# Block 0's attention scores as 18 full bursts instead of 24 bursts of three, two and four chunks

## Chip, cores, metric

One core of a Trainium2 chip runs the whole program. The metric is device time in microseconds (us), the median of several executions. Besides whole-run times I use lengths between two marks in one trace; the text says which.

## The reference, cut to what matters

```python
h   = x + attention(layernorm(x), wqkv, wo)   # S=2048, D=1024, 32 heads of 32, causal window 256
out = h + silu(layernorm(h) @ w1) @ w2        # F=3584
# mask: 0 <= q - k < 256; softmax over k
```

The kernel works on four blocks of 512 queries. A head's scores are computed in chunks of 128 keys by 128 queries. A query tile of a later block sees three key tiles, which makes 12 chunks for four query tiles. Block 0 has nothing before it and only nine: (k,q) = (0,0) (0,1) (0,2) (1,1) (1,2) (1,3) (2,2) (2,3) (3,3).

## The kernel before

TensorE alternates between two kinds of work: the dense projections (Q, K and V) of block b, and the attention of block b-1. Four heads make a group; each head has 32 rows, so a score burst uses TensorE as four row tiles of 32 rows side by side (`tile_position`). It writes two tiles of two banks each (`sc`, one for each pair of heads) in PSUM, the memory that takes the results of matmuls. ScalarE takes exponentials of them into one of 12 buffers, GpSimd zeroes the masked triangles, and a later attention output multiplies by V.

```python
PIECES = {"A": [(0, 0, 3, 0), (-2, 0, 1, 3)],     # (key tile, first query tile, how many, chunk place)
          "B": [(-1, 0, 2, 0), (2, 2, 2, 2)],
          "C": [(3, 3, 1, 0), (1, 1, 3, 1)]}      # block 0 skips key tiles below 0: 3, 2 and 4 chunks

def scores(b, g, kind):
    for kt, q0, nq, ch in PIECES[kind]:
        ...
        for hh in range(4):                       # four heads, four row tiles
            nc.tensor.matmul(sc[hh // 2][:, hh % 2, ch*P:(ch+nq)*P], lhsT=kT..., rhs=qT...,
                             start=True, stop=True, tile_position=(hh * 32, 0))
    for pair in range(2):
        nc.scalar.activation(out=e[:, :, lo:hi], in_=sc[pair][:, :, lo:hi], func=ACT.Exp, scale=scale)
        mask(...)                                 # GpSimd

for g in range(8):                                # 24 places for each block
    for kind in "ABC":
        run_late()
        scores(b - 1, g, kind)
        dense[n]()                                # eight matmuls of 512 columns
        if pending: pending.pop(0)()              # a third of the last group's attention output
        ...
    pending = tail_of(b - 1, g)                   # 5, 6 and 5 of 16 products
```

The softmax here doesn't subtract the row's maximum and nothing guards it: scores larger than these inputs give would overflow.

Of the kernel before, what the change touches and what calls it, by code (L numbers as in the profile page):

```python
# [11 lines left out]
ACT = mybir.ActivationFunctionType  # L12
ALU = mybir.AluOpType

P = 128
# [11 lines left out]
CHUNKS = [  # L27
    [(-2, "A", 3), (-1, "B", 0), (0, "A", 0)],
    [(-1, "B", 1), (0, "A", 1), (1, "C", 1)],
    [(0, "A", 2), (1, "C", 2), (2, "B", 2)],  # L30
    [(1, "C", 3), (2, "B", 3), (3, "C", 0)],
]
KINDS = "ABC"


@with_exitstack
def kernel(
# [10 lines left out]
    nc = tc.nc  # L48
# [6 lines left out]
    DH = D // H  # L55
# [3 lines left out]
    NB = S // 512  # L59
    G = H // 4  # L60
    VW = DH + 1
    scale = float(DH) ** -0.5
# [20 lines left out]
    sc = [sc_pool.tile([P, 2, 512], F32, name=f"sc{i}") for i in range(2)]  # L83
    o_ps = [ps.tile([P, 8, 64], F32, name=f"o_ps{i}") for i in range(2)]
# [23 lines left out]
    qT = [view(r_a, (4096, 8192, 12288, 0)[b], G, 512) for b in range(NB)]  # L108
    kT = [view(r_a, 16384 + 4096 * b, G, 512) for b in range(NB)]
    v = view(r_a, 32768, S // P, H, VW)  # L110
# [4 lines left out]
    ebuf = [view(r_e, 1024 * i, 2, 512) for i in range(12)]  # L115
# [10 lines left out]
    def load_x(b, j):  # L126
        nc.sync.dma_start(out=x_ring[(b % 2) * 4 + j], in_=x2d[(b * 4 + j) * P:(b * 4 + j + 1) * P, :])
# [72 lines left out]
    def ln_tiles(tag):  # L200
        st = small.tile([P, 4, 2], F32, name=f"st_{tag}", tag=f"st_{tag}")
        rs = small.tile([P, 4], F32, name=f"rs_{tag}", tag=f"rs_{tag}")
        return st, rs
# [5 lines left out]
    def next_acc():  # L209
        acc_n[0] += 1  # L210
        return acc_banks[acc_n[0] % len(acc_banks)]

    def v_group(b, j, c, copy):
        acc = next_acc()
        for kt in range(KT):
            nc.tensor.matmul(acc, lhsT=lnT_b[b % 2][:, kt, j * P:(j + 1) * P], rhs=wv[:, kt, c * 512:(c + 1) * 512],  # L216
                             start=(kt == 0), stop=(kt == KT - 1))
        copy(out=v[:, b * 4 + j, c * 16:(c + 1) * 16, 0:DH], in_=acc.rearrange("p (h d) -> p h d", d=DH))

    def qk_group(b, which, g, copy):  # L220
        acc = next_acc()
        col0 = which * D + g * P
        for kt in range(KT):
            nc.tensor.matmul(acc, lhsT=wqk[:, kt, col0:col0 + P], rhs=lnT_b[b % 2][:, kt, :],  # L224
                             start=(kt == 0), stop=(kt == KT - 1))
        copy(out=(qT, kT)[which][b][:, g, :], in_=acc)  # L226
# [7 lines left out]
    late = []  # L234

    def run_late():
        while late:
            late.pop(0)()
# [12 lines left out]
    def e_of(i, kind, pair):  # L251
        return ebuf[(i * 6 + KINDS.index(kind) * 2 + pair) % 12]

    def scores(b, g, kind):
        for kt, q0, nq, ch in PIECES[kind]:
            t = b * 4 + kt
            if t < 0:
                continue
            for hh in range(4):
                r0 = hh * DH  # L260
                nc.tensor.matmul(  # L261
                    sc[hh // 2][:, hh % 2, ch * P:(ch + nq) * P],
                    lhsT=kT[t // 4][r0:r0 + DH, g, (t % 4) * P:(t % 4 + 1) * P],
                    rhs=qT[b][r0:r0 + DH, g, q0 * P:(q0 + nq) * P],
                    start=True, stop=True, tile_position=(r0, 0),
                )
        lo, hi = 0, 512
        if b == 0:
            lo, hi = {"A": (0, 384), "B": (256, 512), "C": (0, 512)}[kind]
        for pair in range(2):  # L270
            e = e_of(b * G + g, kind, pair)
            nc.scalar.activation(out=e[:, :, lo:hi], in_=sc[pair][:, :, lo:hi], func=ACT.Exp, scale=scale)  # L272
            if kind == "A":
                mask(e, 0, 1, True)
                mask(e, 2, 1 if b == 0 else 2, False)
            elif kind == "B":
                if b > 0:
                    mask(e, 1, 1, False)
                mask(e, 2, 1, True)
            else:  # L280
                mask(e, 0, 2, True)
                mask(e, 3, 1, False)

    def mask(e, c0, n, upper):
        ap = e[:, :, c0 * P:(c0 + n) * P].rearrange("p h (c q) -> p h c q", q=P)
        sgn = 1 if upper else -1
        nc.gpsimd.affine_select(out=ap, in_=ap, pattern=[[0, 2], [0, n], [sgn, P]],  # L287
                                compare_op=ALU.is_ge if upper else ALU.is_gt,
                                fill=0.0, base=0, channel_multiplier=-sgn)

    def attn_out(b, g, first, last):
        i = b * G + g
        for n in range(first, last):
            pair, qt, hh = n // 8, n // 2 % 4, n % 2
            chunks = [x for x in CHUNKS[qt] if b * 4 + x[0] >= 0]
            for m, (kt, kind, ch) in enumerate(chunks):
                nc.tensor.matmul(  # L297
                    o_ps[pair][:, qt * 2 + hh, 0:VW],
                    lhsT=e_of(i, kind, pair)[:, hh, ch * P:(ch + 1) * P],
                    rhs=v[:, b * 4 + kt, g * 4 + pair * 2 + hh, :],  # L300
                    start=(m == 0), stop=(m == len(chunks) - 1),
                )
            if n % 8 == 7:
                attn_norm(i, pair)

    def attn_norm(i, pair):
        recip = small.tile([P, 8, 1], F32, name="recip", tag="recip")
        nc.vector.reciprocal(out=recip[:], in_=o_ps[pair][:, :, DH:VW])
        nc.vector.tensor_tensor(
            out=obuf[i % 3][:, :, pair * 64:(pair + 1) * 64].rearrange("p t (h d) -> p t h d", d=DH),  # L310
            in0=o_ps[pair][:, :, 0:DH].rearrange("p (t h) d -> p t h d", h=2),
            in1=recip[:].rearrange("p (t h) o -> p t h o", h=2).to_broadcast([P, 4, 2, DH]), op=ALU.mult,
        )

    def attn_transpose(b, g):
        i = b * G + g
        nc.sync.dma_start_transpose(out=qT[b][:, g, :].rearrange("p (t q) -> p t q", q=P),
                                    in_=obuf[i % 3].rearrange("p t d -> p (t d)"))
# [7 lines left out]
    dve, act = nc.vector.tensor_copy, nc.scalar.copy  # L326
# [24 lines left out]
    def ln1_steps(b):  # L351
        st, rs = ln_tiles("a")
        xs = [x_ring[(b % 2) * 4 + j] for j in range(4)]
        steps = [lambda j=j: ln_stats(xs[j], st, j) for j in range(4)]
        steps += rstd_steps(st, rs)
        for j in range(4):
            steps.append(lambda j=j: ln_norm(xs[j], st, rs, j))
        return steps, [lambda j=j: ln_transpose(xs[j], lnT_b[b % 2], j) for j in range(4)]
# [13 lines left out]
    steps = sum(ln1_steps(1), [])  # L372
# [8 lines left out]
        nc.sync.dma_start(out=w1[:, kt, :], in_=w1_v[:, kt, :])  # L381


    pending = []
    for b in range(1, NB):
        dense = [lambda j=j, c=c: v_group(b, j, c, dve) for j in range(4) for c in range(2)]
        dense += [lambda w=w, g=g: qk_group(b, w, g, dve) for g in range(G) for w in range(2)]
        if b + 1 < NB:
            for j in range(4):
                load_x(b + 1, j)  # L390
            steps, turns = ln1_steps(b + 1)
        else:
            steps, turns = [], []
            nc.sync.dma_start(out=wo[:, 0:4, :], in_=wo_v[:, 0:4, :])
            nc.sync.dma_start(out=wo[:, 4:8, :], in_=wo_v[:, 4:8, :])
            load_res(0)
            load_res(1)
        n = 0
        for g in range(G):
            for kind in KINDS:  # L400
                run_late()
                if b == NB - 1 and n in (4, 10, 14):
                    load_w1({4: 7, 10: 6, 14: 5}[n])
                scores(b - 1, g, kind)
                dense[n]()
                if pending:
                    pending.pop(0)()
                if steps and n >= 1 and n != 3:
                    steps.pop(0)()
                elif turns and n % 3 == 2:  # L410
                    turns.pop(0)()
                n += 1
            pending = tail_of(b - 1, g)
        assert not steps and not turns


    dense = []
# [6 lines left out]
    steps = []  # L424
    n = 0
    for g in range(G):
        for kind in KINDS:
            run_late()
# [8 lines left out]
            if n == 9:  # L437
                steps = ln2_steps(0)
# [7 lines left out]
        pending = tail_of(NB - 1, g)  # L446
# [28 lines left out]
    for b in range(NB):  # L475
        extra = []
        if b == 0:
            extra = [(f, 1) for f in pending]
            pending = []
        for ft in range(FT):  # L480
# [8 lines left out]
            if b == 0 and 6 <= ft < 14:  # L489
                j, c = divmod(ft - 6, 2)  # L490
# [4 lines left out]
        steps = ln2_steps(b + 1) if b + 1 < NB else []  # L495
# [55 lines left out]
```

## Time and profile before

| | before |
|---|---|
| median of 3 executions | 699.61 us (699.46 to 699.77) |
| TensorE busy in the profiled execution | 98% of 697.4 us |
| ScalarE, GpSimd busy | 37%, 25% |
| block 0's scores beside block 1's projections | 51.65 to 108.66 us, 57.01 us |
| first score burst to first MLP matmul | 51.65 to 292.51 us, 240.86 us |

Read the busy shares with care: TensorE's 98% includes the time in which the array changes its mode. Differences of starts in the timeline tell more than lengths, for matmul ends are modelled. The lines are in the prediction.

### The profile page before, as it was taken

Reading aid. Unit: us, or ns where it says so; the run is one execution under the profiler, and the core shown is the slowest. Engines: PE = TensorE matmul, PEld = TensorE weight load, DVE = VectorE, ACT = ScalarE, POOL = GpSimd, SP = SyncE. Lnnn points to the kernel's source line nnn. Section 1 sums busy time; section 2 is a strip of 40 time slices with the busy share of each in tenths; the row PEclk is TensorE's granted clock in tenths of the full one; section 3 lists DMA queues with packets and bytes.
Section 4 is the critical chain, followed back from the end, with each engine's and each line's share of the span. In section 5 each row is a group of like instructions: output and inputs, shape, how many; then the busy total and the mean of one; then the engine's idle time right before and its main releaser. Section 6 shows DMA issues by size and latency. Waiting matters only on the chain.

```text
span 697.4 us, 12171 instructions
## 1 busy us (share of the span) xinstructions
PE 686.6 (98%) x4970; PEld 334.9 (48%) x5059; DVE 286.5 (41%) x608; ACT 259.9 (37%) x335; POOL 172.3 (25%) x375
## 2 busy tenths in 40 slices
PE   8999999999999999999999999999999999999998
PEld 3444555555555555544444444444444444444445
DVE  5446645753444348544425233334144251233111
ACT  4316667777777777621310023300033200233000
POOL 1006566777777777600000000000000000000000
PEclk9999999999999999999999999999999999999999
DMA  9541123025431578881023410023300024100110
GB/s 311 171 73 57 32 55 91 17 49 157 116 122 25 180 228 293 211 296 58 32 75 99 105 39 1 0 77 83 83 1 0 10 92 96 46 1 0 31 39 23
DMA packets 75399, 60.55 MB, mean 87 GB/s; under 512 B 49232, under 2 KB 59472, under 8 KB 75344
## 3 DMA queue, kind: packets, MB, share of 16 engines
q1 hardware_dynamic: 75344, 59.78, 29.7%
q8 instruction: 39, 0.64, 0.4%
q14 instruction: 16, 0.13, 0.1%
HBM read 39.85 MB, written 8.39 MB: 69 GB/s over the span
## 4 chain that ended last, share of the span: by engine, by line
PE 97%; DMA 1%; issue 1%; DVE 0%; ACT 0%; SPq 0%
PE hacc L461 18%; PE hacc L498 17%; PE acc L224 16%; PE acc L498 10%; PE acc L461 9%; PE acc L216 8%; PE acc L243 7%; PE o_ps L297 5%; PE sc L261 4%; PE hacc L243 2%; DMA r_o<-in_A_x_dram 1%; PE o_ps L196 0%; DVE ln_st L158 0%; ACT r_w L197 0%; DVE r_o L179 0%
## 5 line engine op out<-in xcount | busy, mean ns | idle before, releaser
L272 ACT ACTIVATE r_e<-sc 128x1024 bf16<-128x1024 f32 (+2 forms) x192 | 175.8, 967 | 66.1 <-PE sc L261 52.5
L287 POOL TENSOR_SCALAR_AFFINE_SELECT r_e<-r_e 128x256 bf16<-128x256 bf16 (+1 forms) x368 | 169.3, 489 | 120.7 <-ACT r_e L272 117.7
L498 PEld LDWEIGHTS <-r_a 128*128 128x128 bf16 x952 | 90.9, 98 | 103.0
L461 PEld LDWEIGHTS <-r_w 128*128 128x128 bf16 x896 | 87.4, 98 | 104.8
L498 PE MATMUL hacc<-r_a 128*128 128x512 bf16 (+2 forms) x605 | 121.9, 359 | 0.6
L461 PE MATMUL hacc<-r_e,r_w 128*128 128x512 bf16 x444 | 100.2, 379 | 0.6
L470 ACT ACTIVATE r_n<-hacc 128x512 f32<-128x512 f32 x30 | 17.9, 597 | 178.9 <-PE hacc L461 178.9
L224 PEld LDWEIGHTS <-r_w 128*128 128x128 bf16 x512 | 46.1, 98 | 58.6 <-issue 8.9
L498 PE MATMUL acc<-r_a 128*128 128x512 bf16 x328 | 73.6, 379 | 0.4
L226 DVE CAST r_a<-acc 128x512 bf16<-128x512 f32 x56 | 38.7, 691 | 81.3 <-PE acc L224 57.7
L297 PEld LDWEIGHTS <-r_e 128*128 128x128 bf16 x1440 | 50.3, 96 | 22.7
L224 PE MATMUL acc<-r_t,r_w 128*128 128x512 bf16 x240 | 60.0, 380 | 0.8
L224 PE MATMUL acc<-r_w 128*128 128x512 bf16 x246 | 57.7, 380 | 0.5
L297 PE MATMUL o_ps<-r_a,r_e 128*128 128x33 bf16 x1440 | 51.2, 178 | 0.0
L243 PE MATMUL acc<-r_o,r_a 128*128 128x512 bf16 x196 | 48.7, 380 | 0.6
L461 PE MATMUL acc<-r_e,r_w 128*128 128x512 bf16 x216 | 49.1, 379 | 0.0
L243 PEld LDWEIGHTS <-r_a 128*128 128x128 bf16 x256 | 23.1, 98 | 29.6 <-issue 5.1
L261 PE MATMUL sc<-r_a 32*128 32x128 bf16 (+2 forms) x704 | 37.2, 276 | 0.0
L513 DVE SCALAR_TENSOR_TENSOR r_t<-hacc,r_t 128x512 bf16<-128x512 f32 (+2 forms) x22 | 14.0, 635 | 56.4 <-PE hacc L498 56.4
L513 DVE SCALAR_TENSOR_TENSOR r_t<-acc,r_t 128x512 bf16<-128x512 f32 x12 | 8.3, 692 | 64.2 <-PE acc L498 59.7
L471 DVE SCALAR_TENSOR_TENSOR r_a<-r_n,hacc 128x512 bf16<-128x512 f32 x30 | 20.6, 688 | 33.0 <-ACT r_n L470 33.0
L461 PE MATMUL hacc<-r_a,r_w 128*128 128x512 bf16 x141 | 32.7, 379 | 0.2
(65 smaller groups left out, 419.7 us busy)
## 6 DMA issues: line engine op xcount, KB each, us to landing
r_w<-in_B_w_dram SPq DMA_DIRECT2D x8, 896.0 KB, 5.2
r_a<-in_B_w_dram SPq DMA_DIRECT2D x7, 1024.0 KB, 7.8
r_w<-in_A_wqkv_dram SPq DMA_DIRECT2D x6, 1024.0 KB, 11.3
r_o<-in_A_x_dram SPq DMA_DIRECT2D x16, 256.0 KB, 4.2
h_dram<-r_t SPq DMA_DIRECT2D x16, 256.0 KB, 3.2
r_t<-h_dram SPq DMA_DIRECT2D x16, 256.0 KB, 2.8
out_dram<-r_t SPq DMA_DIRECT2D x31, 128.0 KB, 1.7
r_e<-h_dram SPq DMA_DIRECT2D x3, 1024.0 KB, 5.7
```

Of the source, the lines that this page charges most:

```text
L216: nc.tensor.matmul(acc, lhsT=lnT_b[b % 2][:, kt, j * P:(j + 1) * P], rhs=wv[:, kt, c * 512:(c + 1) * 512], start=(kt == 0), stop=(kt == KT ...
L224: nc.tensor.matmul(acc, lhsT=wqk[:, kt, col0:col0 + P], rhs=lnT_b[b % 2][:, kt, :], start=(kt == 0), stop=(kt == KT - 1))
L226: copy(out=(qT, kT)[which][b][:, g, :], in_=acc)
L243: nc.tensor.matmul(acc, lhsT=qT[b][:, g, j * P:(j + 1) * P], rhs=wo[:, g, c * 512:(c + 1) * 512], start=(g == 0), stop=(g == G - 1))
L261: nc.tensor.matmul(sc[hh // 2][:, hh % 2, ch * P:(ch + nq) * P], lhsT=kT[t // 4][r0:r0 + DH, g, (t % 4) * P:(t % 4 + 1) * P], rhs=qT[b][r0 ...
L272: nc.scalar.activation(out=e[:, :, lo:hi], in_=sc[pair][:, :, lo:hi], func=ACT.Exp, scale=scale)
L287: nc.gpsimd.affine_select(out=ap, in_=ap, pattern=[[0, 2], [0, n], [sgn, P]], compare_op=ALU.is_ge if upper else ALU.is_gt, fill=0.0, base ...
L297: nc.tensor.matmul(o_ps[pair][:, qt * 2 + hh, 0:VW], lhsT=e_of(i, kind, pair)[:, hh, ch * P:(ch + 1) * P], rhs=v[:, b * 4 + kt, g * 4 + pa ...
L461: nc.tensor.matmul(acc, lhsT=w1[:, kt, ft * P:(ft + 1) * P], rhs=ln2T[b][:, kt, :], start=(kt == 0), stop=(kt == KT - 1))
L471: nc.vector.scalar_tensor_tensor(out=gT[:, ft, :], in0=th, scalar=1.0, in1=acc, op0=ALU.add, op1=ALU.mult)
L498: nc.tensor.matmul(acc[:, 0:c1 - c0], lhsT=gT[:, ft, j * P:(j + 1) * P], rhs=w2[ft // 4][:, ft % 4, c0:c1], start=(ft == 0), stop=(ft == F ...
L513: nc.vector.scalar_tensor_tensor(out=t_out[j % 2][:, c0:c1], in0=acc[:, 0:c1 - c0], scalar=0.5, in1=t_in[j % 2][:, c0:c1], op0=ALU.mult, o ...
```

## The change

For block 0 alone, the nine chunks of all eight groups form one stream of 72, cut into 18 bursts of four. A burst may hold chunks of two groups. The bursts are spread over the 192 dense matmuls of block 1's projections, one every 10 or 11, so they may fall inside a dense accumulation. The attention output of a group comes in two pieces (one a pair of heads) behind a later burst instead of three behind a dense group. The intent is to fill the score banks.

```diff
+def first_stream(n_groups):
+    for g in range(n_groups):
+        for kt, q in ((0,0),(0,1),(0,2),(1,1),(1,2),(1,3),(2,2),(2,3),(3,3)):
+            if not bursts or len(bursts[-1]) == 4:
+                bursts.append([])
+            ...
 def v_group(...):                                # qk_group likewise
     for kt in range(KT):
+        if between:
+            between()
         nc.tensor.matmul(acc, ...)
+def between():
+    k, m = count
+    if m * len(first_bursts) >= k * 192:
+        run_late()
+        scores_first(k)
+        if pending:
+            pending.pop(0)()
+        for g in range(G):
+            if first_where[g, 3, 3][0] == k:
+                pending.extend([lambda g=g: attn_out_first(g, 0), lambda g=g: attn_out_first(g, 1)])
+        count[0] += 1
+    count[1] += 1
 ...  # cut: scores_first, attn_out_first; the general loop now starts at b = 2
```

More of the change, by code (lines that the diff above doesn't have):

```diff
@@ L33 @@
 KINDS = "ABC"
+def first_stream(n_groups):
+    bursts, where = [], {}
+    for g in range(n_groups):
+        for kt, q in ((0, 0), (0, 1), (0, 2), (1, 1), (1, 2), (1, 3), (2, 2), (2, 3), (3, 3)):
+            if not bursts or len(bursts[-1]) == 4:
+                bursts.append([])
+            where[g, kt, q] = (len(bursts) - 1, len(bursts[-1]))
+            bursts[-1].append((g, kt, q))
+    return bursts, where
 @with_exitstack
@@ L211, in next_acc, with v_group @@
         return acc_banks[acc_n[0] % len(acc_banks)]
-    def v_group(b, j, c, copy):
+    def v_group(b, j, c, copy, between=None):
         acc = next_acc()
         for kt in range(KT):
+            if between:
+                between()
             nc.tensor.matmul(acc, lhsT=lnT_b[b % 2][:, kt, j * P:(j + 1) * P], rhs=wv[:, kt, c * 512:(c + 1) * 512],
@@ L218, in v_group, with qk_group @@
         copy(out=v[:, b * 4 + j, c * 16:(c + 1) * 16, 0:DH], in_=acc.rearrange("p (h d) -> p h d", d=DH))
-    def qk_group(b, which, g, copy):
+    def qk_group(b, which, g, copy, between=None):
         acc = next_acc()
@@ L223, in qk_group @@
         for kt in range(KT):
+            if between:
+                between()
             nc.tensor.matmul(acc, lhsT=wqk[:, kt, col0:col0 + P], rhs=lnT_b[b % 2][:, kt, :],
@@ L252, in e_of @@
         return ebuf[(i * 6 + KINDS.index(kind) * 2 + pair) % 12]
+    first_bursts, first_where = first_stream(G)
     def scores(b, g, kind):
@@ L256, in scores @@
             t = b * 4 + kt
-            if t < 0:
-                continue
             for hh in range(4):
@@ L266, in scores @@
                 )
-        lo, hi = 0, 512
-        if b == 0:
-            lo, hi = {"A": (0, 384), "B": (256, 512), "C": (0, 512)}[kind]
         for pair in range(2):
             e = e_of(b * G + g, kind, pair)
-            nc.scalar.activation(out=e[:, :, lo:hi], in_=sc[pair][:, :, lo:hi], func=ACT.Exp, scale=scale)
+            nc.scalar.activation(out=e, in_=sc[pair], func=ACT.Exp, scale=scale)
             if kind == "A":
                 mask(e, 0, 1, True)
-                mask(e, 2, 1 if b == 0 else 2, False)
+                mask(e, 2, 2, False)
             elif kind == "B":
-                if b > 0:
-                    mask(e, 1, 1, False)
+                mask(e, 1, 1, False)
                 mask(e, 2, 1, True)
@@ L282, in scores, with scores_first @@
                 mask(e, 3, 1, False)
+    def scores_first(n):
+        ch = 0
+        while ch < 4:
+            g, kt, q0 = first_bursts[n][ch]
+            nq = 1
+            while ch + nq < 4 and first_bursts[n][ch + nq] == (g, kt, q0 + nq):
+                nq += 1
+            for hh in range(4):
+                r0 = hh * DH
+                nc.tensor.matmul(
+                    sc[hh // 2][:, hh % 2, ch * P:(ch + nq) * P],
+                    lhsT=kT[0][r0:r0 + DH, g, kt * P:(kt + 1) * P],
+                    rhs=qT[0][r0:r0 + DH, g, q0 * P:(q0 + nq) * P],
+                    start=True, stop=True, tile_position=(r0, 0),
+                )
+            ch += nq
+        for pair in range(2):
+            e = ebuf[(2 * n + pair) % 12]
+            nc.scalar.activation(out=e, in_=sc[pair], func=ACT.Exp, scale=scale)
+            for ch, (g, kt, q) in enumerate(first_bursts[n]):
+                if kt != q - 1:
+                    mask(e, ch, 1, kt == q)
     def mask(e, c0, n, upper):
@@ L294, in attn_out @@
             pair, qt, hh = n // 8, n // 2 % 4, n % 2
-            chunks = [x for x in CHUNKS[qt] if b * 4 + x[0] >= 0]
-            for m, (kt, kind, ch) in enumerate(chunks):
+            for m, (kt, kind, ch) in enumerate(CHUNKS[qt]):
                 nc.tensor.matmul(
@@ L300, in attn_out @@
                     rhs=v[:, b * 4 + kt, g * 4 + pair * 2 + hh, :],
-                    start=(m == 0), stop=(m == len(chunks) - 1),
+                    start=(m == 0), stop=(m == 2),
                 )
@@ L304, in attn_out, with attn_out_first @@
                 attn_norm(i, pair)
+    def attn_out_first(g, pair):
+        for qt in range(4):
+            for hh in range(2):
+                kts = range(max(0, qt - 2), qt + 1)
+                for kt in kts:
+                    n, ch = first_where[g, kt, qt]
+                    nc.tensor.matmul(
+                        o_ps[pair][:, qt * 2 + hh, 0:VW],
+                        lhsT=ebuf[(2 * n + pair) % 12][:, hh, ch * P:(ch + 1) * P],
+                        rhs=v[:, kt, g * 4 + pair * 2 + hh, :],
+                        start=(kt == kts[0]), stop=(kt == qt),
+                    )
+        attn_norm(g, pair)
+        if pair == 1:
+            late.append(lambda: attn_transpose(0, g))
     def attn_norm(i, pair):
@@ L381, in load_w1 @@
         nc.sync.dma_start(out=w1[:, kt, :], in_=w1_v[:, kt, :])
+    for j in range(4):
+        load_x(2, j)
+    steps, turns = ln1_steps(2)
     pending = []
-    for b in range(1, NB):
+    count = [0, 0]
+    def between():
[10 more added lines that the diff above has]
+        count[1] += 1
+    dense = [lambda j=j, c=c: v_group(1, j, c, dve, between) for j in range(4) for c in range(2)]
+    dense += [lambda w=w, g=g: qk_group(1, w, g, dve, between) for g in range(G) for w in range(2)]
+    for n in range(24):
+        dense[n]()
+        if steps and n >= 1 and n != 3:
+            steps.pop(0)()
+        elif turns and n % 3 == 2:
+            turns.pop(0)()
+    assert not steps and not turns and count[0] == len(first_bursts)
+    for b in range(2, NB):
         dense = [lambda j=j, c=c: v_group(b, j, c, dve) for j in range(4) for c in range(2)]
```

## The prediction

> **What bounds the kernel now.** I read the page first: the header row of busy shares, the slices and the chain that ended last.
>
> ```profile
> PE 686.6 (98%) x4970; PEld 334.9 (48%) x5059; DVE 286.5 (41%) x608; ACT 259.9 (37%) x335; POOL 172.3 (25%) x375
> ...
> PE   8999999999999999999999999999999999999998
> ...
> PEclk9999999999999999999999999999999999999999
> ...
> PE 97%; DMA 1%; issue 1%; DVE 0%; ACT 0%; SPq 0%
> ```
>
> TensorE is busy in every slice at full clock, and 97% of the chain is its own work. So nothing that the change takes from ScalarE or GpSimd can shorten the run by itself; only what it takes out of TensorE's stream counts. Since a busy share also contains drains and switches, I next read the timeline of TensorE, which gives the start of each run of equal matmuls, and took differences of starts. The stage that the change touches (block 0's scores beside block 1's projections) runs from the first score matmul at 51.65 us to the first score matmul of the next block at 108.66 us: 57.01 us, 24 places. One head group in the steady part of it:
>
> ```profile
> 72.64 0.34 PE L261 MATMUL sc<-r_a 32*128 32x384 bf16 x4
> 72.92 1.90 PE L224 MATMUL acc<-r_t,r_w 128*128 128x512 bf16 x8
> 74.65 0.38 PE L297 MATMUL o_ps<-r_a,r_e 128*128 128x33 bf16 x9
> 74.97 0.29 PE L261 MATMUL sc<-r_a 32*128 32x256 bf16 x4
> 75.19 1.90 PE L224 MATMUL acc<-r_t,r_w 128*128 128x512 bf16 x7
> 76.92 0.48 PE L297 MATMUL o_ps<-r_a,r_e 128*128 128x33 bf16 x13
> 77.34 0.40 PE L261 MATMUL sc<-r_a 32*128 32x128 bf16 x8
> 77.67 1.90 PE L224 MATMUL acc<-r_t,r_w 128*128 128x512 bf16 x8
> ```
>
> (Columns: start, length, engine, line, operation and tiles; a count of 7 is a missing record.) A place is a score burst, eight dense matmuls of 512 columns, and a piece of the attention output. Dense takes 74.65 - 72.92 = 1.73 us (216 ns a matmul). The bursts take 0.28, 0.22 and 0.33 us until dense starts, for 384, 256 and 512 columns. 128 columns more cost about 0.055 us, which is 128 columns at 2.4 a nanosecond (0.053), so the four row tiles stream side by side, and a constant of about 0.115 us is left over in each burst. The attention pieces take 0.32, 0.42 and 0.44 us for 9, 13 and 14 matmuls. What is constant in them shows where no score burst follows, at the start of the MLP:
>
> ```profile
> 292.51 1.89 PE L461 MATMUL acc<-r_a,r_w 128*128 128x512 bf16 x7
> 294.24 0.53 PE L297 MATMUL o_ps<-r_a,r_e 128*128 128x33 bf16 x15
> 294.62 1.89 PE L461 MATMUL hacc<-r_a,r_w 128*128 128x512 bf16 x8
> 296.34 0.61 PE L297 MATMUL o_ps<-r_a,r_e 128*128 128x33 bf16 x18
> 296.80 1.89 PE L461 MATMUL hacc<-r_a,r_w 128*128 128x512 bf16 x7
> ```
>
> There 15 take 0.38 us and 18 take 0.46 us: 25.4 ns each and nothing constant. So the 0.09 us over 25.4 ns x n that a piece costs ahead of a burst (9 x 25.4 = 0.23 against 0.32) belongs to the burst as well: about 0.09 us to go into the 32-row mode and 0.115 us to come out. Place by place: from 72.64 to 74.97 is 2.33 us = 1.73 dense + 0.16 score columns + 0.23 attention + 0.21 rest; the next is 2.37 = 1.73 + 0.107 + 0.33 + 0.20. The early places, which have no attention, give the same: 2.05 us from the burst at 53.76 to that at 55.81, less 1.73 and 0.107, is 0.21. **Each burst costs about 0.205 us beyond its columns**, whichever engine work stands between.
>
> One place is different, the third to fourth burst, before any attention output exists:
>
> ```profile
> 56.14 1.90 PE L216 MATMUL acc<-r_w,r_t 128*128 128x512 bf16 x8
> 57.98 0.60 PE L261 MATMUL sc<-r_a 32*128 32x384 bf16 x4
> 58.51 1.90 PE L216 MATMUL acc<-r_w,r_t 128*128 128x512 bf16 x8
> ```
> ```profile
> 56.24 1.94 ACT L272 ACTIVATE r_e<-sc 128x1024 bf16<-128x1024 f32 x2 [1.08 <-PE sc L261]
> ```
>
> This burst took 58.51 - 57.98 = 0.53 us instead of 0.28. The exponentials of the full burst before it ended at 56.24 + 1.94 = 58.18, and the list of weight loads shows the burst's last one at 58.24: TensorE waited some 0.25 us for the second score bank. It is the only such wait that I found in the stage. As a check the stage sums to 24 x 1.733 + 3.84 (8 x 1152 columns / 2400) + 252 attention matmuls x 0.0254 = 6.40 + 0.25 + 24 x 0.205 = 4.92: 57.0 us against 57.01 measured.
>
> **What the Trainium skill says.** "TensorEngine Tiling (Array Packing)", Key Properties: changing the tiling mode, not merely the tile, drains TensorE. The trace agrees: the constant stands around score bursts alone (0.205 us) and not around attention pieces (0). "TensorE: Matmul & The Clock Gate", Part 1: warm matmuls follow one another after N / 2.4 plus about 2.5 ns, never under about 25 ns. The trace has 216 ns for 512 columns and 25.4 ns for 33, so an attention matmul costs the floor. "ScalarE: Activation LUTs", What ACT_TABLE_LOAD costs: an ACTIVATE costs a fixed part plus 0.833 ns an element, and back-to-back ones overlap by about 93 ns. The groups by form show 1021, 808 and 594 ns for 1024, 768 and 512 elements: 0.834 ns an element and 167 ns fixed, so 12 fewer spare about 2 us of ScalarE, less with overlap.
>
> **The change, part by part.**
> *Bursts.* 72 chunks of 128 columns for 8 groups fill 18 bursts of 4 instead of 24 of 3, 2 and 4. Score columns are the same (72 x 128 = 9216). Six mode switches in and out go: 6 x 0.205 = 1.23 us, all on TensorE's path.
> *Pieces.* Run through by hand, the stream cuts into 42 pieces of four matmuls where there were 32: 40 matmuls and 40 loads more; the built program agrees, with 80 more instructions on TensorE. The two-piece burst (128 then 384 columns, 0.33 us) already shows no charge beyond its columns, so I put the further pieces at 0; six bursts have three pieces, and 20 ns each would be 0.1 us.
> *The wait.* The first bursts now stand after 11, 11 and 10 dense matmuls instead of 8. Ten take 2.16 us, the mode switch adds 0.09, and ScalarE is done 0.10 to 0.18 + 1.94 = 2.04 to 2.12 us after the burst. So the 0.25 us should go, with about 0.15 us to spare. The same distance without attention between recurs only once later, from burst 11 to 12.
> *Attention output.* 16 pieces of 18 matmuls for 24 of 9, 13 and 14: the same 36 a group, no constant cost, 0. In the stage fall 14 pieces = 252 matmuls as before; group 7's pass into the next block's places, as before. The order is now scores, attention, dense; the switch back is paid in front of attention instead of dense.
> *Beside TensorE.* GpSimd: 96 one-chunk masks (423 ns) for 64 + 16 double ones (640 ns): 40.6 us instead of 37.3 of the 57. ScalarE: the same 36864 elements a lane in 36 instead of 48 instructions, some 34 us. VectorE: the same copies, norms and steps.
> Sum: -1.23 - 0.25 = -1.48 us, so the stage becomes 55.5 us, and the whole 699.61 - 1.48 = 698.13 us. Everything after it is paced by TensorE and starts that much earlier.
>
> **The rivals.**
> *GpSimd becomes the wait.* A group's attention output now may start one burst after its last scores, not a place later. Worst case, three masks a pair: 0.14 (ScalarE's start) + 0.97 + 0.12 + 3 x 0.423 = 2.5 us for the first pair. Attention follows at the earliest 2.16 + 0.09 + 0.33 = 2.6 us after the burst, 3.0 where attention stood in between. The two tight spots, group 0 and group 4, have their last chunk as the first of the burst, so they need only the first mask. I expect no wait; if all eight first pieces waited 0.2 us, 1.6 us would go and the time would stay at 699.7.
> *Cutting into an accumulation costs.* Bursts now fall inside a group of eight dense matmuls. If resuming cost 50 ns in 18 places, the gain would shrink by 0.9 us to give 699.0. Against: the switch back is followed by a fresh weight load either way.
> *The switch is dearer in front of attention.* Its matmuls are short and hide no load: 14 x 30 ns = 0.4 us, 698.5. No place before has that order, so this is untested.
> *VectorE lags.* Six dense groups stand without a burst, 1.73 us after the last. A copy (0.69) plus statistics (1.48) or a norm of the attention (0.62) fit twice over in the two groups that a bank may wait, so no gain is lost.
> *More is won.* If attention pieces had a constant of their own after all, 7 fewer in the stage (21 to 14) at 0.09 us would add 0.6 us and give 697.5. The MLP lines speak against it.
>
> **Range and chances.** The six switches are nearly sure; unsure are the 0.25 us wait, the order in front of attention and the three-piece bursts, together perhaps 0.6 us upwards, 0.5 downwards; the three timed runs span 0.3 us. I take 698.15 us, 697.4 to 698.9. A change of 2% would be 14 us, a quarter of the stage, and nothing in the sum is of that size.
>
> **What would show it.** In the profile after: 18 bursts with 0.33 us from burst to the next 128-row matmul; the stage at 55.5 us; no burst of 0.5 us; attention 18 in 0.46 us; 180 exponentials, all of 1024; score bursts waiting for ScalarE, or attention waiting for GpSimd, in no place over 0.1 us. The prediction is wrong if TensorE shows gaps ahead of attention pieces, if the first dense matmul after an attention piece comes late, or if the stages after 108 us change their length.

## The result

The changed kernel took **698.34 us** (698.15 to 698.6, 6 executions) against 699.69 us of the kernel before in the same series (its highest, 702.72, included). The ratio is 0.9974, 95% interval 0.9957 to 0.9991. The difference of medians, 1.35 us, is 0.2%: small, but real.

The page of the changed kernel, TensorE's row and the chain's shares by engine:

```profile
PE 690.6 (99%) x5099; PEld 332.1 (48%) x5099; DVE 288.1 (41%) x608; ACT 258.5 (37%) x323; POOL 175.2 (25%) x391
...
PE 98%; DMA 1%; DVE 0%; ACT 0%; SPq 0%; issue 0%
```

The bound is the same. TensorE's busy time rose by 4 us although the span fell by 1 us. That is no contradiction but a trap: the trace before holds 4970 matmul records to 5059 weight loads, the trace after 5099 to 5099. Missing records make an engine look less busy. ScalarE has 12 instructions fewer, GpSimd 16 more, as forecast.

The timeline of TensorE after, at the third to fifth burst (line 305 is now the score matmul, 230 the dense one, 346 the attention output):

```profile
57.40 0.40 PE L305 MATMUL sc<-r_a 32*128 32x128 bf16 x8
57.73 2.33 PE L230 MATMUL acc<-r_w,r_t 128*128 128x512 bf16 x10
59.99 0.40 PE L305 MATMUL sc<-r_a 32*128 32x384 bf16 x8
60.32 0.62 PE L346 MATMUL o_ps<-r_a,r_e 128*128 128x33 bf16 x18
60.79 2.54 PE L230 MATMUL acc<-r_w,r_t 128*128 128x512 bf16 x11
63.26 0.40 PE L305 MATMUL sc<-r_a 32*128 32x128 bf16 x12
63.59 0.62 PE L346 MATMUL o_ps<-r_a,r_e 128*128 128x33 bf16 x18
```

Take differences of starts. Each burst lasts 0.33 us to the next 128-row matmul, also the last one, which has three pieces (12 matmuls): more pieces cost nothing. The fourth burst, which lasted 0.53 us before, lasts 0.33. The attention piece of 18 takes 0.47 us, close to the 0.46 forecast. The burst at 59.99 stands at the start of a dense group and the one at 63.26 inside one, and both are alike: breaking into an accumulation costs nothing that shows.

The stage runs from 51.78 to 107.42 us, 55.64 us instead of 57.01: 1.37 us less. To the MLP's first matmul at 291.50 us it is 239.72 us instead of 240.86, only 1.14 us less. So 0.23 us were lost after the stage. The place is the first four bursts of the next block (line 277 after, line 261 before), after first:

```profile
112.09 0.61 PE L346 MATMUL o_ps<-r_a,r_e 128*128 128x33 bf16 x18
112.64 0.40 PE L277 MATMUL sc<-r_a 32*128 32x128 bf16 x8
112.97 1.90 PE L230 MATMUL acc<-r_w 128*128 128x512 bf16 x8
114.80 0.73 PE L277 MATMUL sc<-r_a 32*128 32x384 bf16 x8
115.47 1.90 PE L230 MATMUL acc<-r_w 128*128 128x512 bf16 x8
```
```profile
113.15 1.94 ACT L285 ACTIVATE r_e<-sc 128x1024 bf16<-128x1024 f32 x2 [0.68 <-PE sc L277]
```

and before:

```profile
111.04 0.52 PE L261 MATMUL sc<-r_a 32*128 32x256 bf16 x8
111.49 1.90 PE L216 MATMUL acc<-r_w 128*128 128x512 bf16 x8
...
115.71 0.51 PE L297 MATMUL o_ps<-r_a,r_e 128*128 128x33 bf16 x14
116.16 0.40 PE L261 MATMUL sc<-r_a 32*128 32x384 bf16 x8
116.49 1.90 PE L216 MATMUL acc<-r_w 128*128 128x512 bf16 x8
```

After the change the fourth burst of block 1 lasts 115.47 - 114.80 = 0.67 us instead of 0.33. The last group of block 0 now leaves two attention pieces for the next block instead of three. The third place therefore has none, and the next burst comes 1.83 us after dense began, while ScalarE is done with the banks only at 113.15 + 1.94 = 115.09 us. The kernel before had a smaller wait here: its second burst, behind a short piece of nine, lasted 111.49 - 111.04 = 0.45 us, 0.12 more than the 0.33 of the others. That wait went. The net is 0.34 - 0.12 = +0.22 us.

### The profile page after: what moved, and what is told of

Same layout as the page of the kernel before. It is cut to its first block, busy times and chain, and to the rows that moved or that the text cites. A ratio compares the mean times of both kernels' runs of the same rounds, so it can differ in the third digit from the quotient of the medians.

```text
span 696.4 us, 12339 instructions
## 1 busy us (share of the span) xinstructions
PE 690.6 (99%) x5099; PEld 332.1 (48%) x5099; DVE 288.1 (41%) x608; ACT 258.5 (37%) x323; POOL 175.2 (25%) x391
## 4 chain that ended last, share of the span: by engine, by line
PE 98%; DMA 1%; DVE 0%; ACT 0%; SPq 0%; issue 0%
PE hacc L540 19%; PE hacc L577 17%; PE acc L240 16%; PE acc L577 10%; PE acc L540 9%; PE acc L230 8%; PE acc L259 7%; PE o_ps L331 4%; PE sc L277 3%; PE hacc L259 1%; PE o_ps L346 1%; PE sc L305 1%; DMA r_o<-in_A_x_dram 1%; PE o_ps L208 0%; DVE ln_st L170 0%; ACT r_w L209 0%
## 5 line engine op out<-in xcount | busy, mean ns | idle before, releaser
L322 POOL TENSOR_SCALAR_AFFINE_SELECT r_e<-r_e 128x256 bf16<-128x256 bf16 (+1 forms) x384 | 172.3, 479 | 116.7 <-ACT r_e L314 65.9
L285 ACT ACTIVATE r_e<-sc 128x1024 bf16<-128x1024 f32 x144 | 139.5, 1021 | 45.1 <-PE sc L277 31.0
L331 PEld LDWEIGHTS <-r_e 128*128 128x128 bf16 x1152 | 39.6, 96 | 17.0
L314 ACT ACTIVATE r_e<-sc 128x1024 bf16<-128x1024 f32 x36 | 34.9, 1021 | 21.2 <-PE sc L305 20.1
L331 PE MATMUL o_ps<-r_a,r_e 128*128 128x33 bf16 x1152 | 40.2, 178 | 0.0
```

What stands on the lines that cost most here:

```text
L285: nc.scalar.activation(out=e, in_=sc[pair], func=ACT.Exp, scale=scale)
L314: nc.scalar.activation(out=e, in_=sc[pair], func=ACT.Exp, scale=scale)
L322: nc.gpsimd.affine_select(out=ap, in_=ap, pattern=[[0, 2], [0, n], [sgn, P]], compare_op=ALU.is_ge if upper else ALU.is_gt, fill=0.0, base ...
L331: nc.tensor.matmul(o_ps[pair][:, qt * 2 + hh, 0:VW], lhsT=e_of(i, kind, pair)[:, hh, ch * P:(ch + 1) * P], rhs=v[:, b * 4 + kt, g * 4 + pa ...
```

## The experiments

Eight kernels ran in ten runs, all correct, each run with four to six executions beside the kernel before. Whole-run times scatter, because the start before the first score burst does: it came at 51.6 to 53.9 us in the traces. The length from the first score burst to the first MLP matmul is far steadier: three traces of the changed kernel gave 239.72 us each. After that mark every trace without an edit in the MLP needs 404.8 to 404.9 us. The table gives the median of the whole run and this length, with the length's difference against the changed kernel. The length of the kernel before is from its only trace; its medians in these rounds were 699.22 to 699.56 us.

| kernel | whole run, median us | first burst to MLP, us | against the changed kernel |
|---|---|---|---|
| before | 699.22 | 240.86 | +1.14 |
| changed | 698.10 | 239.72 | 0 |
| 24 bursts of three | 699.29 | 241.06 | +1.34 |
| 24 bursts of 3, 2, 4 | 702.13 | 243.55 | +3.83 |
| three last pieces | 698.07 | 239.45 | -0.27 |
| attention ahead of scores | 698.16 | 239.79 | +0.07 |
| early bursts close together | 699.30 | 240.35 | +0.63 |
| useless 32-row bursts in the MLP | 720.50 | 239.72 | (after the mark) |
| useless 128-row pairs in the MLP | 707.56 | 239.72 | (after the mark) |

### The yardstick

No edit.

> The changed kernel once more, unaltered, as the yardstick of this series. Every theory expects what was measured before, 698.3 us, about 1.35 us below the kernel before.

Measured 698.10 us (698.05 to 699.18), ratio 0.9987 (0.9975 to 1.0). The difference of medians is 1.12 us here, 1.35 in the first series; the traces say 1.14.

### 24 bursts of three chunks

```diff
-            if not bursts or len(bursts[-1]) == 4:
+            if not bursts or len(bursts[-1]) == 3:
...          # loops over the burst's real size; the exponential over size * 128 columns
```

> The stream of the changed kernel cut into 24 bursts of three chunks, one before every eighth dense matmul; exponentials over 384 columns a head instead of 512. Theory (each burst costs a constant of about 0.205 us): six bursts more give +1.23 us over the changed kernel, 699.55 us, and no wait for ScalarE anywhere in block 0, as 1.51 us of exponentials fit into 1.83 us. Rival (the gain came from the waits for the score banks that the wider spacing took away, or from cutting the fixed parts of 12 exponentials): three-chunk bursts do not wait either, so the first gives 698.3; the second gives back all the gain, 699.7, but with ScalarE idle between bursts I expect nothing from it.

Measured 699.29 us, 1.19 more than the changed kernel. In the trace the stage takes 56.92 us against 55.64: 1.28 us for six bursts, **0.213 us each**. No burst in it lasts over 0.28 us, so nothing waits. Three of them:

```profile
57.95 0.34 PE L306 MATMUL sc<-r_a 32*128 32x384 bf16 x4
58.22 0.62 PE L347 MATMUL o_ps<-r_a,r_e 128*128 128x33 bf16 x18
...
60.51 0.34 PE L306 MATMUL sc<-r_a 32*128 32x384 bf16 x4
60.79 0.62 PE L347 MATMUL o_ps<-r_a,r_e 128*128 128x33 bf16 x18
...
63.07 0.34 PE L306 MATMUL sc<-r_a 32*128 32x256 bf16 x8
63.35 1.90 PE L231 MATMUL acc<-r_w,r_t 128*128 128x512 bf16 x8
```

The number of bursts carries the difference between these two kernels. The rival by waits falls: this kernel has no waits in block 0 and is still as slow as the kernel before. The rival by ScalarE's work expected about this time too, for there are 48 exponentials again; it falls by the trace and not by the time, since no burst waits for ScalarE.

### 24 bursts of three, two and four

```diff
-            if not bursts or len(bursts[-1]) == 4:
+            sizes = [3, 2, 4]
+            if not bursts or len(bursts[-1]) == sizes[(len(bursts) - 1) % len(sizes)]:
```

> The same stream cut into bursts of three, two and four chunks in turn, which are the bursts of the kernel before, but with the attention output in two pieces of 18, as in the changed kernel. 24 bursts as in the run with three chunks, so the burst constant gives the same +1.23 us. But every four-chunk burst is now followed by eight dense matmuls with no attention piece before the next burst, 1.83 us against the 2.1 us that ScalarE needs. Theory: eight waits of about 0.25 us, +2.0 us more, 701.5 us. If waits for the score banks were of no account, the time would be that of the run with three chunks, 699.55 us.

Measured 702.13 us, 2.84 more than with bursts of three; between the marks of the traces it is 243.55 - 241.06 = 2.49 us more. The timeline around one four-chunk burst (line numbers shift by one; PEld is the weight load):

```profile
71.44 1.90 PE L241 MATMUL acc<-r_t,r_w 128*128 128x512 bf16 x8
71.62 1.94 ACT L315 ACTIVATE r_e<-sc 128x1024 bf16<-128x1024 f32 x2 [1.56 <-PE sc L306]
...
73.27 0.68 PE L306 MATMUL sc<-r_a 32*128 32x384 bf16 x4
...
73.61 0.09 PEld L306 LDWEIGHTS <-r_a 32*128 32x128 bf16 x1 [0.25 <-issue]
...
73.88 0.62 PE L347 MATMUL o_ps<-r_a,r_e 128*128 128x33 bf16 x18
```

The exponentials end at 71.62 + 1.94 = 73.56, the last weight load of the burst follows at 73.61, and the burst lasts 0.61 us instead of 0.28. It is a wait for the second score bank, and the profile files it under "issue", not under ScalarE. All seven such bursts in the stage wait (0.25 to 0.33 us), and so does the first of block 1. I had expected 0.25 us for each; most are 0.33, and the eight sum to about 2.5 us, which is the difference between the marks. So with these small bursts the attention piece between a full burst and the next had covered ScalarE, and the new schedule could drop it only because it spaces the bursts wider.

### The last group's attention in three pieces

```diff
-        pending.extend([lambda g=g: attn_out_first(g, 0), lambda g=g: attn_out_first(g, 1)])
+        if g == G - 1:   # names shortened; 12 matmuls each: query tiles 0-2 | 3, and 0-1 of the other pair | 2-3
+            pending.extend([first_12, middle_12, last_12])
+        else: ...        # as before
```

> The changed kernel, but the attention output of block 0's last group falls in three pieces of 12 matmuls on the first three places of the next block instead of two of 18 on two. In the changed kernel's trace the fourth burst of that block took 0.67 us instead of 0.33, because the third place has no attention piece and ScalarE is late. Theory: that wait of 0.34 us goes; 8 dense and 12 attention matmuls take 1.73 + 0.30 + 0.09 = 2.12 us against ScalarE's 2.04 to 2.12, so up to 0.05 us of it comes back at each of three bursts: 0.2 to 0.34 us below the changed kernel, 698.05 us. Rival (the longer burst is no wait for ScalarE but a start-up cost of the new block): no change, 698.3, with a long fourth burst still there.

Measured 698.07 us (697.73 to 700.03): by whole-run times nothing against the yardstick. Its trace showed 0.27 us less, so I ran both again.

> The changed kernel unaltered, a third time, as the partner of the next run on the same chip. All theories: 698.1 to 698.4 us; in the trace 239.72 us from the first score burst to the first MLP matmul, as in each trace of it so far.

> The kernel with the last group's attention output in three pieces once more, since its whole-run times of the first series (698.07 against 698.10 us) did not resolve what its trace showed (239.45 against 239.72 us from the first score burst to the MLP). Theory: 0.27 us below its partner, 697.9 us, and the same 239.45 us in the trace; the start before the first burst, which differed by up to 2.3 us between traces, stays as scatter. Rival (the 0.27 us is scatter too): the trace gives 239.7 us.

Measured 698.18 us for the changed kernel (ratio 0.9986, 0.9974 to 0.9999) and **697.79 us** for this one (ratio 0.9976, 0.9964 to 0.9988). The traces repeat themselves to the last digit: 239.72 and 239.45 us. The bursts two to four of block 1, in its timeline:

```profile
109.79 0.44 PE L277 MATMUL sc<-r_a 32*128 32x256 bf16 x8
110.16 1.90 PE L230 MATMUL acc<-r_w 128*128 128x512 bf16 x8
...
114.75 0.43 PE L277 MATMUL sc<-r_a 32*128 32x384 bf16 x8
115.12 1.90 PE L230 MATMUL acc<-r_w 128*128 128x512 bf16 x8
```

The second and the fourth take 0.37 us each instead of 0.33 and 0.67: the wait of 0.34 us is gone and two of 0.04 us came back. The start-up rival falls. By its trace this version beats both kernels. The intervals of the two ratios overlap, so its whole-run lead of 0.39 us is not shown by times alone.

### Attention ahead of the scores

```diff
             run_late()
+            if pending:
+                pending.pop(0)()
             scores_first(k)
-            if pending:
-                pending.pop(0)()
```

> The changed kernel with the attention piece ahead of the score burst, as in the kernel before, instead of behind it. Theory (the mode switch costs the same whichever 128-row matmul follows): 698.3 us, within 0.15. Rival of the prediction (the switch is dearer in front of the short attention matmuls, 14 times 30 ns): 0.4 us less, 697.9. A wait for GpSimd would show as a late first attention matmul; the first pair's masks are done at most 2.5 us after the burst, the piece now comes at 2.16 + 0.46 = 2.6 us, so none is expected.

Measured 698.16 us, and 239.79 us in the trace, +0.07: the order hardly matters. The stage takes 55.71 us. Inside it, one piece of 18 is late:

```profile
75.94 0.61 PE L346 MATMUL o_ps<-r_a,r_e 128*128 128x33 bf16 x18
76.47 0.40 PE L305 MATMUL sc<-r_a 32*128 32x128 bf16 x12
...
78.97 0.79 PE L346 MATMUL o_ps<-r_a,r_e 128*128 128x33 bf16 x18
79.69 0.40 PE L305 MATMUL sc<-r_a 32*128 32x384 bf16 x8
```

The first takes 0.53 us, the second 0.72. The second needs all three masks of the burst before it, and in this order it starts 78.97 - 76.47 = 2.50 us after that burst began; in the changed kernel it is 79.47 - 76.09 = 3.38 us. The sum in the expectation missed this: it put 0.46 us of attention between burst and piece, and in this order none stands there. The 0.19 us is a wait for GpSimd's masks. The profile names no releaser, but the records of the third mask and of the piece's weight loads show it:

```profile
79.02 0.41 POOL L322 TENSOR_SCALAR_AFFINE_SELECT r_e<-r_e 128x256 bf16<-128x256 bf16 x1
```
```profile
79.25 0.12 PEld L346 LDWEIGHTS <-r_e 128*128 128x128 bf16 x2
79.49 0.17 PEld L346 LDWEIGHTS <-r_e 128*128 128x128 bf16 x4
```

The third mask ends at 79.43 (GpSimd's times are rough), the last four loads start at 79.49, and no other attention piece of this trace has such a gap inside it. Without the wait the stage would be 55.52 us, 0.12 us below the changed kernel's 55.64. So the changed order seems to cost about 0.01 us for each of its 14 pieces, an estimate from this difference, and it buys time for the masks.

### The first bursts close together again

```diff
-        if m * len(first_bursts) >= k * 192:
+        if m >= (8 * k if k < 4 else (k * 192 + 17) // 18):
```

> The changed kernel, but its second, third and fourth bursts stand after 8 dense matmuls each instead of 11, 11 and 10; everything later is as before. No attention piece lies between these. Theory: each of the three bursts waits for ScalarE, 2.04 to 2.12 us plus the signal against 1.73 + 0.1 us, so about 0.3 us each: +0.9 us, 699.2 us, with three bursts of 0.6 to 0.7 us in the trace. Rival (the long fourth burst of the kernel before was something of its own and not spacing): 698.3.

Measured 699.30 us and +0.63 us in the trace. The second burst:

```profile
53.04 1.69 PE L230 MATMUL acc<-r_w,r_t 128*128 128x512 bf16 x7
54.87 0.65 PE L305 MATMUL sc<-r_a 32*128 32x256 bf16 x8
55.45 1.90 PE L230 MATMUL acc<-r_w,r_t 128*128 128x512 bf16 x8
```

The three bursts last 0.58, 0.50 and 0.54 us, which is 0.25 + 0.17 + 0.21 = 0.63 us over 0.33. The spacing makes the wait. I expected 0.9. My reading of the rest, which no run tests by itself: a late burst lets ScalarE start on the first pair of heads before the second is finished (at 55.46, only 0.01 us after dense begins, instead of 0.10), so consecutive waits shorten one another.

### The mode switch by itself, and its control

The same two matmuls with 32 and with 128 rows (`o_ps_flat` stands for the two idle attention banks):

```diff
         acc = h1_group(b, ft)
+        if b > 0:
+            for hh in range(2):        # control: all 128 rows, no tile_position
+                r0 = 32 * hh
+                nc.tensor.matmul(o_ps_flat[hh][:, 0:128], lhsT=w1[r0:r0 + 32, 0, 0:128],
+                                 rhs=ln2T[b][r0:r0 + 32, 0, 0:128], start=True, stop=True, tile_position=(r0, 0))
```

> The changed kernel with a useless burst in the MLP of blocks 1 to 3: after each of 84 groups of eight dense matmuls, two 32-row matmuls of 128 columns into the two idle attention banks; nobody waits for them. Theory: each costs the constant of about 0.205 us plus 0.053 us of columns, 84 x 0.258 = 21.7 us, 720.0 us. Rival (the constant at a score burst is a wait for another engine or a semaphore, not the mode): 84 x 0.06 = 5 us, 703.3 us.

> The control to the useless 32-row bursts: in the same 84 places two 128-row matmuls of 128 columns into the same banks, so no change of mode. Both theories: 84 x 2 x 0.056 = 9.4 us, 707.7 us. The theory of the mode switch expects the 32-row form to be the slower one by some 12 us although it streams half as long; its rival expects it to be the faster one.

Measured 720.50 and 707.56 us. From the MLP's first matmul to the end the traces need 427.26 and 414.20 us against 404.88, so each of the 84 additions costs 22.38 / 84 = 0.266 us with 32 rows and 9.32 / 84 = 0.111 us with 128. One of each, the 32-row form first:

```profile
403.06 1.89 PE L540 MATMUL hacc<-r_e,r_w 128*128 128x512 bf16 x8
404.88 0.23 PE L564 MATMUL o_ps<-r_e,r_w 32*128 32x128 bf16 x2
405.04 1.90 PE L540 MATMUL hacc<-r_e,r_w 128*128 128x512 bf16 x8
```
```profile
403.32 1.89 PE L540 MATMUL hacc<-r_e,r_w 128*128 128x512 bf16 x8
405.05 0.28 PE L563 MATMUL o_ps<-r_e,r_w 128*128 128x128 bf16 x2
405.16 1.03 PE L540 MATMUL hacc<-r_e,r_w 128*128 128x512 bf16 x4
```

Going in shows as the later start: 1.82 us after dense instead of 1.73, 0.09 us. Coming out takes 0.16 us, of which 0.053 us are the 128 columns, so about 0.11 us. The two rows stream side by side in half the control's time, and still the form costs 2.4 times as much. Less its columns it costs 0.266 - 0.053 = **0.213 us**, the same as a score burst, in a place where no other engine has a result for it or wants one. The rival that the constant is a wait for another engine falls.

What makes up the constant stays open. The weight loads differ too, the 32-row form first:

```profile
404.88 0.09 PEld L564 LDWEIGHTS <-r_w 32*128 32x128 bf16 x2 [0.42 <-issue]
```
```profile
404.83 0.31 PEld L563 LDWEIGHTS <-r_w 128*128 128x128 bf16 x2
```

The control's first load starts 405.05 - 404.83 = 0.22 us ahead of its matmul, while that of the 32-row form starts only with its matmul, after 0.42 us in which the loader stood idle. No run tells a drain of the array from a load that could not run ahead.

## Why the prediction was right

The measured 698.34 us lies within 0.2 us of the 698.15 predicted and in the range. That it is so close is partly luck: a gain of 1.48 us was predicted, the medians differ by 1.35, 1.12 and 1.38 us in three series, and the traces, the better measure, show 1.14. One thing on its list of what would show it failed: a score burst waited more than 0.1 us for ScalarE (0.34 us in block 1). One of its signs of being wrong came: the stages after 108 us changed their length, by 0.23 us. The main mechanism, fewer switches, was right; by its own steps:

- *Bursts.* Shown. Six switches were put at 1.23 us, from 0.205 each; the run with bursts of three gives 1.28 us, 0.213 each, and the useless bursts give 0.213 once more.
- *Pieces.* Shown by the trace: a burst with three pieces lasts 0.33 us like those with two.
- *The wait.* The 0.25 us of the fourth burst went, and setting the bursts close brought three such waits back.
- *Attention output.* Two slips. First, "the switch back is paid in front of attention instead of dense" was booked at 0. The kernel before and the one with bursts of three have 24 bursts each; their stages are 57.01 and 56.92 us, a difference of 0.09 where the vanished wait alone would make 0.25. So 0.16 us went to the new arrangement. The run with attention ahead of the scores puts about 0.12 us of it on the order; the rest stays open. Second, "group 7's pass into the next block's places, as before" was the step that failed: 36 matmuls pass as before, but in two pieces instead of three, and the place without one made a wait of 0.34 us in block 1 where the kernel before had 0.12. The prediction had looked at how ScalarE fits only inside the stage, so its "Everything after it is paced by TensorE" did not hold there.
- *Beside TensorE.* Right. ScalarE's and GpSimd's extra or spared work moved nothing: GpSimd released attention pieces twice in the stage, together 0.4 us on the weight loader, but those pieces (at 60.32 and 88.60) take 0.47 and 0.46 us like the others, and their bursts 0.33. The sum of ScalarE's time is a little low: 36 exponentials of 1021 ns are 36.8 us, with their overlap 34.9 in the trace, and not "some 34".
- *Rivals.* GpSimd as a wait, the broken accumulation, a lagging VectorE and "More is won" did not come. The switch that is dearer in front of attention came at about a third of its size, some 0.12 us of 0.4.

The sum, against -1.48 predicted: -1.28 switches, -0.25 wait, +0.16 arrangement make -1.37 us in the stage; +0.22 in the next block makes -1.15 us, and the traces differ by 1.14.

## What to carry to other kernels

Count the changes of TensorE's tiling mode: here each visit to the 32-row mode cost 0.21 us on top of its columns, so one wider visit beats two narrow ones even if no column is saved. When you regroup work, check the places just behind the changed stage: pieces that are handed over also serve as spacing for another engine. When the gain is below the scatter of whole runs, compare two marks inside the traces; here they repeated to 0.01 us where run times differed by 2 us.

## What the Trainium skill lacked or had wrong

- "TensorEngine Tiling (Array Packing)", Key Properties, says that a change of tiling mode drains TensorE but gives no cost. Here in and out together cost 0.213 us, about 0.09 of it going in and 0.11 coming out, with two row tiles as with four. How much of it is the drain is not shown.
- "TensorE: Matmul & The Clock Gate", Back-to-back issue gap, gives a sustained figure of about 131 ns for a stream of weight loads and 512-column matmuls and 81 ns for 128 columns. No run here shows either: 512 columns followed one another at 216 ns, and the control's pairs of 128 columns at 0.111 / 2 = 56 ns. The same page's form N / 2.4 + 2.5 fits both.
- "Perfetto Trace Analysis", Identifying Dependency Chains, mentions that an instruction that waits for several engines may get a separate semaphore instruction ahead of it, but not what that costs. In the changed kernel 24 of block 0's 36 exponentials have one, first at 70.0 us, and that is where the first buffer of 12 comes round again. In the burst before, the next work of TensorE begins at 66.85 us and ScalarE 0.10 us after it; in that one it begins at 69.90 and ScalarE 0.19 us after it:

```profile
L314 ACT ACTIVATE r_e<-sc x36: 1017/1022/1025, 52.2 to 105.8; 128x1024 bf16<-128x1024 f32 x36
L314 ACTq EVENT_SEMAPHORE  x24: 38/38/38, 70.0 to 104.9; - x24
```

  (Columns: shortest, median and longest ns, first and last start.) This would explain why waits for the banks were 0.25 us early and 0.33 us later. No run took the second semaphore away, so it is not shown.
